# Retention and a routed mixture of experts on one core: the table of slots holds a row number instead of five bfloat16 values

## The chip, the cores and the metric

The kernel runs on one core of a Trainium2 chip. The metric is the device time of one execution in microseconds (us): the median of three timed runs. The profile is one further execution of the same program, recorded by the hardware profiler. Engines are named as the profile names them: PE is TensorE, DVE is VectorE, ACT is ScalarE, POOL is GpSimd, SP is SyncE.

## The reference

Four sequences of 768 tokens go through a retention with 8 heads of 64 columns. Its output, 3072 rows of 512, is the input `x` of a mixture of 8 experts, each with a first product to 1024 columns and a second one back to 512. A noisy gate chooses two experts for every token.

```python
for t in range(S):                                   # retention, per batch and head
    state = gamma * state + outer(k[t], v[t])
    y[t] = scale * q[t] @ state
x = y.transpose(0, 2, 1, 3).reshape(3072, 512)
noisy = x @ w_gate + log1p(exp(x @ w_noise)) * noise
top2 = the two largest of noisy, per token
top2_w = exp(top2_l - max); top2_w /= top2_w.sum(-1) + 1e-09
for e in range(8):
    for k in range(2):
        mask = top2[:, k] == e
        h = maximum(x[mask] @ w1[e], 0)
        out[mask] += top2_w[mask, k] * (h @ w2[e])
```

## The kernel before, in words

**Order of the work.** The order in which the kernel's code issues instructions is the order in which each engine executes them: nothing is moved by a scheduler. An engine that waits for an operand holds everything behind it in its own queue. SP's queue carries most DMAs and the transposes by DMA; POOL's queue carries the indirect DMAs.

**Retention.** It works on 24 chunks of 128 tokens, six per sequence. A chunk's output is scaled by a power of two and split into two float16 parts (`x_split`), which are transposed by DMA for the gate (L346) and written as one row per token to a table in DRAM, `xbuf` (L347: 1024 float16, 2,048 bytes a row).

**Routing.** Each sequence is routed in steps `route_a` to `route_h`, spread over the following chunks; the last sequence has no chunks behind it, and beside its routing stand only the units of expert 0's first list (`early`). The result is a table of slots. An expert has up to seven blocks of 128 slots, and each slot names a token and its gate weight. To fill the table, every token and each of its two choices becomes a one-hot row of lanes (`a`, L470), a one-hot row of blocks (`ob`, L468), and the product `bb` of `ob` with five bfloat16 values `vv`: the token number in two parts and the weight in three (L478). `route_f` sums a^T bb over the tokens on PE into 5 x 56 columns (L485), and `acc` collects them over the sequences. `slots` makes the token `tk`, the row index `idx` and the weight `wacc` from it. `ranks` orders experts 1 to 7 by their number of tokens and permutes `tk` and `wacc`.

**Experts.** For each block, `gather` (L591, on POOL) brings the 128 rows named by `idx` from `xbuf` into one of four buffers `xg`, and `x_t` (L598, on SP) transposes them into `xe`. A first product (`mm1`, "unit" below: 12 matmuls, L672 to L674, for 128 of the 1024 columns and half of the tokens) goes into one of three PSUM buffers `pH`; ACT takes its upper part `hh` (L675), and DVE the rest `hl` (L676), which is the last reader of the buffer. There are sixteen units an expert. Then `mm2` follows block by block (L702 to L704); ACT scales its rows with the gate weight times the inverse scales, `gse` (L688), and `put` (L693, on POOL) adds them to `out` in DRAM by an indirect DMA. Every put waits until the put before it has landed.

**Beside an expert.** While expert e is in its second product, the gathers and transposes of expert e+1 are issued, one block ahead of each `mm2` (for expert 0, the last four units of its first product also take one each). The weights of e+1 are loaded, measured (`w_sum`), scaled (`w_scale`) and split into a high part on ACT (`w_hi`, L192) and a low part on DVE (`w_lo`, L197). Beside expert 0's second product also stand `route_g` and `loop_table` (L534 to L572): tables for a loop at the end, over tokens beyond an expert's slots.

Of the kernel before, what the change touches and what calls it, by code (L numbers as in the profile page):

```python
# [32 lines left out]
# fullest with the most slots.  What exceeds an expert's slots goes through the loop at the end.  # L33
# [23 lines left out]
def _constants():  # L57
# [34 lines left out]
def moe_kernel(ctx, tc, qT, kT, kt, vt, noise, wgn, w1, w2, ctab, qtab, xbuf, out):  # L92
# [9 lines left out]
    # keeps the tensor engine's clock up while the first operands come in  # L102
# [21 lines left out]
    zero = consts.tile([128, DM], F32, name="zero")  # L124
    posb = consts.tile([128, NCH, NL], F32, name="posb")       # place in the list, BIG if not chosen
    gateb = consts.tile([128, NCH, NL], F32, name="gateb")
    acc = consts.tile([128, NV, NCOL], F32, name="acc")    # slots: token + 1 in two parts, weight in three
    wacc = consts.tile([128, NCOL], F32, name="wacc")
    lanes = consts.tile([128, 128], BF, name="lanes")
    blks = consts.tile([128, NCOL], BF, name="blks")  # L130
# [13 lines left out]
    LST = pR[:, 160:160 + NV * NCOL].rearrange("p (v n) -> p v n", v=NV)  # L144
# [18 lines left out]
    def w_load(e, which, i, n=1):  # L163
        # n quarters from the ith on
# [78 lines left out]
    def zero_out(i):  # L243
        # the output and the rows of padding start as zeros
        if i < 6:
            nc.sync.dma_start(out[128 + i * 512:128 + (i + 1) * 512, :].rearrange("(p r) d -> p r d", p=128),
                              zero[:, None, :].to_broadcast([128, 4, DM]))
        else:
            nc.sync.dma_start(out[:128, :], zero)
# [39 lines left out]
    def q_table(c):  # L289
        # the decay of chunk c's queries, out of chunk 0's  # L290
# [48 lines left out]
    def x_split(j, eng=None):  # L339
# [7 lines left out]
        nc.sync.dma_start(xbuf[128 + j * C:128 + (j + 1) * C, :], x.rearrange("p a d -> p (a d)"))  # L347
# [27 lines left out]
    def route_b(b):  # L375
        # noisy logits, the two largest
# [21 lines left out]
        R[b] = (oh, mb, den)  # L398

    def route_c(b):  # L400
        # places in the lists
        oh, mb, den = R[b]
# [6 lines left out]
        g = work.tile([128, 2, NC], F32, name="g")  # L409
# [12 lines left out]
        nc.vector.tensor_tensor(g[:, 1], den, g[:, 0], op=OP.mult)
        R[b] = (oh, g, gr, cb, vv)

    def route_h(b):
        oh, g, gr, cb, vv = R[b]
        nc.vector.tensor_copy(vv[:, :, :, 2], g)
        nc.vector.tensor_tensor(gr, g, vv[:, :, :, 2], op=OP.subtract)
        nc.vector.tensor_copy(vv[:, :, :, 3], gr)
        nc.vector.tensor_tensor(vv[:, :, :, 4], gr, vv[:, :, :, 3], op=OP.subtract)  # L430

    def route_d(b):
        oh, g, gr, cb, vv = R[b]
# [22 lines left out]
        lf = work.tile([128, 2, 2, NC], BF, name="lf")  # L456
        nc.vector.tensor_copy(lf, lb)
        R[b] = (oh, g, ps, lf, vv)

    def route_e(b, k):  # L460
        # the slots' tokens and weights as sums of one-hot products
        if k == 0:
            R[b] += (work.tile([128, 2, NC, 128], BF, name="a", bufs=1),
                     work.tile([128, 2, NC, NV, NCOL], BF, name="bb", bufs=1),
                     work.tile([128, 2, NC, NCOL], BF, name="ob", bufs=1))
        oh, g, ps, lf, vv, a, bb, ob = R[b]
        s3 = [128, NC, NCOL]
        nc.vector.tensor_tensor(ob[:, k], blks[:, None, :].to_broadcast(s3), lf[:, 1, k, :, None].to_broadcast(s3),  # L468
                                op=OP.is_equal)
        nc.vector.tensor_tensor(a[:, k], lanes[:, None, :].to_broadcast([128, NC, 128]),  # L470
                                lf[:, 0, k, :, None].to_broadcast([128, NC, 128]), op=OP.is_equal)
        # the last sequence's are waited for: GpSimd takes a part
        m = 3 if b == B - 1 else NV
# [7 lines left out]
    def route_f(b):  # L481
# [458 lines left out]
```

## Time and profile before

| | |
|---|---|
| median of three runs | 727.25 us |
| lowest and highest of them | 721.35 us, 729.62 us |
| span of the profiled execution | 733.5 us |
| PE busy | 685.0 us, 93% of the span, 4789 instructions |
| DVE busy | 294.0 us, 40%, 719 instructions |
| ACT busy | 311.0 us, 42% |
| POOL busy | 237.9 us, 32% |
| bytes moved by DMA | 119.09 MB |

The page gives no other time of the profiled execution than its span. "Busy" counts an instruction's time on its engine, without waits. A group row of the page reads: line, engine, operation, output <- inputs, count | busy us, mean ns of one | idle time just before, and what ended most of it. A timeline row reads: start in us, duration in us, engine, line, operation, tiles, count, and in brackets the wait before and what ended it. Rows that start with two numbers joined by a colon are stretches of the span.

### The profile page before, as it was taken

What the parts mean: (1) busy time and instruction counts of PE and PEld (TensorE: products, weight loads), DVE (VectorE), ACT (ScalarE), POOL (GpSimd) and SP (SyncE); (2) the same over time, 40 slices, a digit from 0 to 9 for tenths busy, and PEclk for the clock granted to TensorE, in tenths of its full rate; (3) what the DMA queues carried; (4) which work ended last, traced back from release to release, by engine and by line L of the source; (5) the groups of instructions that cost most, each with busy time, mean ns of one, the idle gap of its engine ahead of it and who ended that gap; (6) DMA issues with size and microseconds to landing.
All of it is one profiled execution on the core that took longest, in us unless ns stands there. A gap on an engine that the chain in (4) does not pass through costs nothing.

```text
span 733.5 us, 12009 instructions
## 1 busy us (share of the span) xinstructions
PE 685.0 (93%) x4789; PEld 431.0 (59%) x4789; DVE 294.0 (40%) x719; ACT 311.0 (42%) x562; POOL 237.9 (32%) x186
## 2 busy tenths in 40 slices
PE   8879879889879999999999999999999999999991
PEld 6879769777448555455546545654555466446540
DVE  3326778695942573215221521432152225216100
ACT  4554444447204374344443534443444435344110
POOL 4564734652333220431033123304321421240021
PEclk9997787986999999999999999999999999999997
DMA  9999955995869953467367826744673685353032
GB/s 331 260 296 245 290 181 165 294 294 146 303 115 248 216 163 130 88 115 221 84 115 120 267 45 119 182 155 86 116 218 85 122 177 185 68 104 60 11 47 30
DMA packets 116057, 119.09 MB, mean 162 GB/s; under 512 B 82560, under 2 KB 82816, under 8 KB 112416
## 3 DMA queue, kind: packets, MB, share of 16 engines
q1 hardware_dynamic: 104080, 91.25, 45.0%
q0 software_dynamic: 11344, 26.22, 19.4%
q10 hardware_dynamic: 576, 0.84, 0.4%
q8 instruction: 38, 0.62, 0.4%
q14 instruction: 19, 0.16, 0.1%
HBM read 72.67 MB, written 26.21 MB: 135 GB/s over the span
## 4 chain that ended last, share of the span: by engine, by line
PE 76%; DVE 8%; DMA 7%; ACT 3%; issue 2%; POOL 1%; SPq 1%; POOLq 0%; ACTq 0%
PE pH L672 11%; PE pH L673 11%; PE pH L674 11%; PE pO L702 10%; PE pO L704 10%; PE pO L703 10%; PE pY L320 3%; DMA xt<-x 3%; PE pA L306 2%; PE pY L316 2%; PE pU L324 1%; DMA wst<-w 1%; DVE am L309 1%; DVE bb L478 1%; DMA xe<-xg 1%
## 5 line engine op out<-in xcount | busy, mean ns | idle before, releaser
L693 POOL DMA_INDIRECT out<-ot,idx x54 | 84.9, 1573 | 360.2 <-ACT ot L688 214.4
L672 PE MATMUL pH<-xe,w1h 128*128 128x384 f16 (+4 forms) x544 | 176.6, 325 | 3.9 <-DMA xe<-xg 3.3
L673 PE MATMUL pH<-xe,w1h 128*128 128x384 f16 (+4 forms) x544 | 176.5, 324 | 0.0
L674 PE MATMUL pH<-xe,w1l 128*128 128x384 f16 (+4 forms) x544 | 176.4, 324 | 0.0
L676 DVE SCALAR_TENSOR_TENSOR hl<-pH,hh 128x384 f16<-128x384 f32 (+4 forms) x136 | 74.4, 549 | 210.5 <-ACT hh L675 209.7
L704 PE MATMUL pO<-w2h,hl 128*128 128x512 f16 x384 | 145.5, 379 | 0.0
L703 PE MATMUL pO<-w2l,hh 128*128 128x512 f16 x384 | 145.5, 379 | 0.0
L702 PE MATMUL pO<-w2h,hh 128*128 128x512 f16 x384 | 145.5, 379 | 0.0
L675 ACT ACTIVATE hh<-pH 128x384 f16<-128x384 f32 (+4 forms) x136 | 65.7, 483 | 127.1 <-PE pH L674 125.2
L688 ACT ACTIVATE ot<-pO,gse 128x512 f32<-128x512 f32 (+4 forms) x54 | 37.0, 686 | 173.8 <-PE pO L704 169.3
L197 DVE SCALAR_TENSOR_TENSOR w1l<-wst,wsc,w1h 128x1024 f16<-128x1024 f32 x32 | 42.7, 1339 | 106.8 <-ACT w1h L192 106.8
L672 PEld LDWEIGHTS <-w1h 128*128 128x128 f16 x544 | 54.2, 100 | 34.5 <-DMA xe<-xg 1.7
L673 PEld LDWEIGHTS <-w1h 128*128 128x128 f16 x544 | 53.5, 98 | 35.4 <-issue 2.8
L674 PEld LDWEIGHTS <-w1l 128*128 128x128 f16 x544 | 53.5, 98 | 34.5 <-issue 0.3
L175 ACT ACTIVATE junk<-wst 128x1024 bf16<-128x1024 f32 x64 | 67.1, 1049 | 5.6 <-DMA wst<-w 2.8
L704 PEld LDWEIGHTS <-hl 128*128 128x128 f16 x384 | 37.5, 98 | 45.8 <-DVE hl L676 0.5
L702 PEld LDWEIGHTS <-hh 128*128 128x128 f16 x384 | 38.1, 99 | 44.1
L703 PEld LDWEIGHTS <-hh 128*128 128x128 f16 x384 | 37.5, 98 | 44.2
L591 POOL DMA_INDIRECT xg<-xbuf,idx x54 | 54.7, 1014 | 25.9 <-issue 14.9
L320 PE MATMUL pY<-vp,am 128*128 128x64 f32 x384 | 60.4, 292 | 0.0
L320 PEld LDWEIGHTS pY<-vp,am 128*128 128x128 f32 x384 | 58.1, 220 | 0.6 <-issue 0.2
L344 POOL TENSOR_TENSOR x<-xs,x 128x512 f16<-128x512 f32 x23 | 32.3, 1405 | 58.6 <-issue 32.3
(163 smaller groups left out, 778.1 us busy)
## 6 DMA issues: line engine op xcount, KB each, us to landing
wst<-w SPq DMA_DIRECT2D x28, 1024.0 KB, 9.2
in_q<-qT SPq DMA_DIRECT2D x24, 256.0 KB, 3.7
in_k<-kT SPq DMA_DIRECT2D x24, 256.0 KB, 4.2
in_v<-vt SPq DMA_DIRECT2D x24, 256.0 KB, 4.9
in_kt<-kt SPq DMA_DIRECT2D x24, 256.0 KB, 5.0
xbuf<-x SPq DMA_DIRECT2D x24, 256.0 KB, 2.6
out<-zero SPq DMA_DIRECT2D x6, 1024.0 KB, 12.6
wst<-w SPq DMA_DIRECT2D x8, 512.0 KB, 7.6
```

The lines of the kernel that those rows point to most:

```text
L175: nc.scalar.activation(junk, st[:, i * 1024:(i + 1) * 1024], AF.Square, accum_out=ss[:, i:i + 1])
L320: nc.tensor.matmul(pY[:, 2 * i + s, :], AM[j][:, s, i, :], VP[j][:, 2 * i + s, :], start=(not c and i == 0 and s == 0), stop=True, skip_gr ...
L591: nc.gpsimd.indirect_dma_start(out=x[:n], out_offset=None, in_=xbuf[:128 + B0 * S] if e == 0 and t < 3 else xbuf, in_offset=bass.IndirectO ...
L672: nc.tensor.matmul(p[:, :n], whi, xh, start=(k == 0), stop=False)
L673: nc.tensor.matmul(p[:, :n], whi, xl, start=False, stop=False)
L674: nc.tensor.matmul(p[:, :n], wlo, xh, start=False, stop=(k == KT - 1))
L675: nc.scalar.activation(hh[:, f, n0:n1], p[:, :n], AF.Relu)
L676: nc.vector.scalar_tensor_tensor(hl[:, f, n0:n1], p[:, :n], 0.0, hh[:, f, n0:n1], op0=OP.max, op1=OP.subtract)
L693: nc.gpsimd.indirect_dma_start(out=out, out_offset=bass.IndirectOffsetOnAxis(ap=idx[:n, i:i + 1], axis=0), in_=ot[:n], in_offset=None, com ...
L702: nc.tensor.matmul(p, a, WT["2h"][:, f, :], start=(f == 0), stop=False)
L703: nc.tensor.matmul(p, a, WT["2l"][:, f, :], start=False, stop=False)
L704: nc.tensor.matmul(p, c, WT["2h"][:, f, :], start=False, stop=(f == FT - 1))
```

## The change

The table of slots now holds one float16 number per slot: the token's row, as a constant of the kernel (token minus 1536, plus 1 where that is not negative, so that no token has 0). `ob` is the one-hot of blocks times that number, made by one tensor_scalar per chunk; `a` likewise is one tensor_scalar per chunk. The values `vv`, the product `bb`, `wacc`, `acc` and the table `gateb` are gone, and the matmuls of `route_f` have 56 columns instead of 280.

The weights take another way. A row of `xbuf` gets four more float32 numbers behind x: the token's two gate weights and its two experts' numbers, so that a row has 2,064 bytes. `route_h` writes them for a sequence with one DMA on SP. A gather brings them along with x, and a new step, `weight`, compares the two expert numbers with the block's expert and sums the weights that match; it is one DVE instruction per block, issued in `x_t` behind the transpose. `out_scale` reads its result `gw` where it read `wacc`.

```diff
-NV = 5
+XW = DM + 4
...
     def route_h(b):
-        oh, g, gr, cb, vv = R[b]
-        nc.vector.tensor_copy(vv[:, :, :, 2], g)
-        nc.vector.tensor_tensor(gr, g, vv[:, :, :, 2], op=OP.subtract)
-        nc.vector.tensor_copy(vv[:, :, :, 3], gr)
-        nc.vector.tensor_tensor(vv[:, :, :, 4], gr, vv[:, :, :, 3], op=OP.subtract)
+        oh, mb, den, i8, g, dn, cb = R[b]
+        nc.vector.tensor_tensor(g[:, :, 0], dn, invx[:, b * NC:(b + 1) * NC], op=OP.mult)
+        nc.vector.tensor_tensor(g[:, :, 1], den, g[:, :, 0], op=OP.mult)
+        nc.vector.tensor_copy(g[:, :, 2:4], i8[:, :, 0:2])
+        if b >= B0:
+            l8 = work.tile([128, NC, 2], F32, name="l8")
+            nc.vector.tensor_scalar(l8, g[:, :, 2:4], float(E), -float(E), op0=OP.is_equal, op1=OP.mult)
+            nc.vector.tensor_tensor(g[:, :, 2:4], g[:, :, 2:4], l8, op=OP.add)
+        nc.sync.dma_start(xbuf[128 + b * S:128 + (b + 1) * S, DM:].rearrange("(c p) d -> p c d", p=128), g)
...
     def route_e(b, k):
-        nc.vector.tensor_tensor(ob[:, k], blks[:, None, :].to_broadcast(s3), lf[:, 1, k, :, None].to_broadcast(s3),
-                                op=OP.is_equal)
-        nc.vector.tensor_tensor(a[:, k], lanes[:, None, :].to_broadcast([128, NC, 128]),
-                                lf[:, 0, k, :, None].to_broadcast([128, NC, 128]), op=OP.is_equal)
...
-                eng.tensor_tensor(bb[:, k, :, v], ob[:, k, :, None, :].to_broadcast(s4),
-                                  vv[:, k, :, v, None].to_broadcast(s4), op=OP.mult)
+        for c in range(NC):
+            nc.vector.tensor_scalar(ob[:, k, c], blks, lf[:, 1, k, c:c + 1], row[:, b * NC + c:b * NC + c + 1],
+                                    op0=OP.is_equal, op1=OP.mult)
+        for c in range(NC):
+            nc.vector.tensor_scalar(a[:, k, c], lanes, lf[:, 0, k, c:c + 1], None, op0=OP.is_equal)
...
-        x = XP[0].tile([128, 2 * DM], F16, name="xg", bufs=4)
+        x = XP[0].tile([128, XW], F32, name="xg", bufs=4)
...
+    def weight(x, n, ef, out):
+        g = x[:n, DM:]
+        t = work.tile([128, 2], F32, name="wt2")
+        nc.vector.scalar_tensor_tensor(t[:n], g[:, 2:4], ef[:n], g[:, 0:2], op0=OP.is_equal, op1=OP.mult,
+                                       accum_out=out[:n])
...
     def x_t(e, t):
         o, n, i = block(e, t)
-        nc.sync.dma_start_transpose(XE[e][:, :, o:o + n], XG.pop((e, t))[:n])
+        x = XG.pop((e, t))
+        nc.sync.dma_start_transpose(XE[e][:, :, o:o + n], x[:n, :DM].bitcast(F16))
+        if t == 0:
+            GW[e] = work.tile([128, NBLK], F32, name="gw")
+            nc.gpsimd.memset(GW[e], 0.0)
+        weight(x, n, eidf[:, e:e + 1], GW[e][:, t:t + 1])
...
-        nc.vector.tensor_scalar(GS[e][:, n0:n1], wacc[:, NBLK * e + n0:NBLK * e + n1], i2, None, op0=OP.mult)
+        nc.vector.tensor_scalar(GS[e][:, n0:n1], GW[e][:, n0:n1], i2, None, op0=OP.mult)
```

Beside this, `rows_of` has one instruction more (the sign), `ranks` permutes `tk` alone and keeps the experts' numbers in float32 (`eidf`) for `weight`, `route_g` makes one table instead of two, `loop_table` has one cast more, and the loop at the end takes its weights from the gathered rows too.

The first place is DVE's order from expert 1 to expert 2, before. `hl` is the first product's rest, the four small instructions behind it are the weights' scale, `w1l` the low part of expert 2's weights; the three `hl` at the end are the first of expert 2.

```order
L676 SCALAR_TENSOR_TENSOR hl<-pH,hh 128x416 x8
L181 TENSOR_REDUCE s_3357<-pR 128x1
L152 TENSOR_SCALAR p2m<-s_3357 128x1
L153 TENSOR_SCALAR wsc_3141<-p2m 128x1
L155 TENSOR_SCALAR wsc_3141<-p2m 128x1
L197 SCALAR_TENSOR_TENSOR w1l<-wst_3139,wsc_3141,w1h 128x1024 x4
L676 SCALAR_TENSOR_TENSOR hl<-pH,hh 128x416 x3
```

The same place after the change, from behind the weights' scale on. `wt` and `gw` are the outputs of `weight`, which reads the gathered rows `xg`.

```order
L580 SCALAR_TENSOR_TENSOR wt_3434,gw<-xg,eidf 128x2
L580 SCALAR_TENSOR_TENSOR wt_3468,gw<-xg,eidf 128x2
L198 SCALAR_TENSOR_TENSOR w1l<-wst_3204,wsc_3206,w1h 128x1024
L580 SCALAR_TENSOR_TENSOR wt_3503,gw<-xg,eidf 128x2
L198 SCALAR_TENSOR_TENSOR w1l<-wst_3204,wsc_3206,w1h 128x1024
L580 SCALAR_TENSOR_TENSOR wt_3539,gw<-xg,eidf 128x2
L198 SCALAR_TENSOR_TENSOR w1l<-wst_3204,wsc_3206,w1h 128x1024
L580 SCALAR_TENSOR_TENSOR wt_3575,gw<-xg,eidf 128x2
L198 SCALAR_TENSOR_TENSOR w1l<-wst_3204,wsc_3206,w1h 128x1024
L580 SCALAR_TENSOR_TENSOR wt_3610,gw<-xg,eidf 128x2
L580 SCALAR_TENSOR_TENSOR wt_3644,gw<-xg,eidf 48x2
L669 SCALAR_TENSOR_TENSOR hl<-pH,hh 128x416 x3
```

Seven instructions that read a gathered block now stand between the last `hl` of expert 1 and the first of expert 2, among the four `w1l`.

The second place is DVE's order in the last sequence's routing, before, for its two lists: `lf` holds every token's lane and block, and `acc` collects the table.

```order
L457 CAST lf<-lb 128x24
L468 TENSOR_TENSOR ob<-blks,lf 128x336
L470 TENSOR_TENSOR a<-lanes,lf 128x768
L478 TENSOR_TENSOR bb<-ob,vv 128x6x168
L676 SCALAR_TENSOR_TENSOR hl<-pH,hh 128x384 x2
L468 TENSOR_TENSOR ob<-blks,lf 128x336
L470 TENSOR_TENSOR a<-lanes,lf 128x768
L478 TENSOR_TENSOR bb<-ob,vv 128x6x168
L490 TENSOR_TENSOR acc<-acc,pR 128x280
```

The same place after the change, up to the first weights of expert 0's second list:

```order
L456 CAST lf<-lb 128x24
L467 TENSOR_SCALAR ob<-blks,lf,ct 128x56 x6
L470 TENSOR_SCALAR a<-lanes,lf 128x128 x6
L669 SCALAR_TENSOR_TENSOR hl<-pH,hh 128x384 x2
L467 TENSOR_SCALAR ob<-blks,lf,ct 128x56 x6
L470 TENSOR_SCALAR a<-lanes,lf 128x128 x6
L481 TENSOR_TENSOR tk<-tk,pR 128x56
L487 TENSOR_SCALAR padv<-tk,ct 128x4
L488 SCALAR_TENSOR_TENSOR padv<-tk,padv 128x4
L489 SCALAR_TENSOR_TENSOR idx<-tk,padv 128x4
L580 SCALAR_TENSOR_TENSOR wt_2446,gw<-xg,eidf 128x2
```

Three wide instructions a list have become twelve small ones, and instructions that read gathered rows follow `idx`.

The third place is SP's order behind the last chunk, before: its transpose and its row write, the fills of `out` with zeros, and the transposes of expert 0's second list.

```order
L346 DMA_TRANSPOSE xt<-x_2069 128x8x128
L347 DMA xbuf<-x_2069 128x1024
L246 DMA out<-zero 512x1x512 x6
L249 DMA out<-zero 128x512
L598 DMA_TRANSPOSE xe<-xg 128x8x128 x3
```

After the change:

```order
L347 DMA_TRANSPOSE xt<-x_2108 128x8x128
L348 DMA xbuf<-x_2108 128x1024
L429 DMA xbuf<-g 128x6x4
L247 DMA out<-zero 512x1x512 x6
L250 DMA out<-zero 128x512
L586 DMA_TRANSPOSE xe<-xg 128x8x128 x3
```

The write of the last sequence's weights and expert numbers (`g`) stands ahead of the fills.

More of the change, by code (lines that the diff above doesn't have):

```diff
@@ L73, in _constants @@
     put("tok1", np.arange(NCH)[None, :] * C + p[:, None] + 1)
-    tv = np.zeros((128, NCH, 2))
-    tv[:, :, 0], tv[:, :, 1] = p[:, None] + 1, np.arange(NCH)[None, :] * C
-    put("tokv", tv.reshape(128, NCH * 2))
+    tk = np.arange(NCH)[None, :] * C + p[:, None] - N // 2
+    put("row", np.where(tk < 0, tk, tk + 1))
     put("pad", p[:, None] - 127)
+    put("lane", p[:, None] - (127 + N // 2))
     put("i64", np.arange(64)[None, :])
@@ L123, in moe_kernel @@
     onef = consts.tile([128, 128], F32, name="onef")
-    zero = consts.tile([128, DM], F32, name="zero")
+    zero = consts.tile([128, DM + 4], F32, name="zero")
     posb = consts.tile([128, NCH, NL], F32, name="posb")
[L126 to L130, printed above, removed]
+    tk = consts.tile([128, NCOL], F32, name="tk")
+    lanes = consts.tile([128, 128], F16, name="lanes")
+    blks = consts.tile([128, NCOL], F16, name="blks")
     idx = consts.tile([128, NCOL], I32, name="idx")
@@ L246, in zero_out @@
             nc.sync.dma_start(out[128 + i * 512:128 + (i + 1) * 512, :].rearrange("(p r) d -> p r d", p=128),
-                              zero[:, None, :].to_broadcast([128, 4, DM]))
+                              zero[:, None, :DM].to_broadcast([128, 4, DM]))
         else:
-            nc.sync.dma_start(out[:128, :], zero)
+            nc.sync.dma_start(out[:128, :], zero[:, :DM])
     gss = work.tile([128, 1], F32, name="gss")
@@ L397, in route_b @@
         nc.vector.tensor_tensor(den, m8[:, :, 1], m8[:, :, 0], op=OP.subtract)
-        R[b] = (oh, mb, den)
+        R[b] = (oh, mb, den, i8)
     def route_c(b):
-        oh, mb, den = R[b]
+        oh, mb, den, i8 = R[b]
         nc.scalar.activation(den, den, AF.Exp)
@@ L481, in route_f @@
+        oh, ps, lf, a, ob = R[b]
+        row = K("row")
+        for c in range(NC):
[3 more added lines that the diff above has]
+            nc.vector.tensor_scalar(a[:, k, c], lanes, lf[:, 0, k, c:c + 1], None, op0=OP.is_equal)
     def route_f(b):
-        oh, g, ps, lf, vv, a, bb, ob = R[b]
+        oh, ps, lf, a, ob = R[b]
         for k in range(2):
@@ L484, in route_f @@
             for c in range(NC):
-                nc.tensor.matmul(LST, a[:, k, c, :], bb[:, k, c], start=(k == 0 and c == 0),
+                nc.tensor.matmul(LST, a[:, k, c, :], ob[:, k, c], start=(k == 0 and c == 0),
                                  stop=(k == 1 and c == NC - 1), skip_group_check=True)
         if b == 0:
-            nc.vector.tensor_copy(acc, LST)
+            nc.vector.tensor_copy(tk, LST)
         else:
-            nc.vector.tensor_tensor(acc, acc, LST, op=OP.add)
-    tk = consts.tile([128, NCOL], F32, name="tk")
@@ L494, in slots, with rows_of @@
-    def slots(n0, n1):
-        nc.vector.tensor_tensor(tk[:, n0:n1], acc[:, 0, n0:n1], acc[:, 1, n0:n1], op=OP.add)
-        if n0 < NBLK:
-            rows_of(tk, n0, n1)
-        nc.vector.tensor_tensor(wacc[:, n0:n1], acc[:, 3, n0:n1], acc[:, 4, n0:n1], op=OP.add)
-        nc.vector.tensor_tensor(wacc[:, n0:n1], wacc[:, n0:n1], acc[:, 2, n0:n1], op=OP.add)
-    def rows_of(tk, n0, n1):
+            nc.vector.tensor_tensor(tk, tk, LST, op=OP.add)
+    def rows_of(n0, n1):
         padv = work.tile([128, NCOL], F32, name="padv")
-        nc.vector.tensor_scalar(padv[:, n0:n1], tk[:, n0:n1], 0.0, K("pad"), op0=OP.is_equal, op1=OP.mult)
-        nc.vector.scalar_tensor_tensor(idx[:, n0:n1], tk[:, n0:n1], 127.0, padv[:, n0:n1], op0=OP.add, op1=OP.add)
+        t, u = tk[:, n0:n1], padv[:, n0:n1]
+        nc.vector.tensor_scalar(u, t, 0.0, K("lane"), op0=OP.is_equal, op1=OP.mult)
+        nc.vector.scalar_tensor_tensor(u, t, 0.0, u, op0=OP.is_lt, op1=OP.add)
+        nc.vector.scalar_tensor_tensor(idx[:, n0:n1], t, float(127 + N // 2), u, op0=OP.add, op1=OP.add)
@@ L570, in loop_table @@
         nc.vector.tensor_scalar(le, loop_e, float(E), -float(E), op0=OP.is_equal, op1=OP.mult)
[L571 removed]
+        nc.vector.tensor_tensor(loop_x, loop_e, le, op=OP.add)
+        nc.vector.tensor_copy(loop_i[:, :64], loop_x)
         nc.vector.tensor_copy(loop_i[:, 64:65], cs[:, NL - 1:NL])
@@ L626, in moe_kernel @@
         at(NC * (B0 + 1) + 2 + t // 2, x_t, 0, t)
-    at(1, nc.sync.dma_start, xbuf[:128, :], zero.bitcast(F16))
+    at(1, nc.sync.dma_start, xbuf[:128, :], zero)
+    at(1, nc.vector.memset, eidf[:, 0:1], 0.0)
     v_scale(0)
@@ L872, in moe_kernel @@
         for c in range(NCH):
-            nc.tensor.matmul(pl, a[:, c, :], rr[:, c, :], start=(c == 0), stop=(c == NCH - 1))
+            nc.tensor.matmul(pl[:, 0:1], a[:, c, :], K("tok1")[:, c:c + 1], start=(c == 0), stop=(c == NCH - 1))
         pv = work.tile([128, 2], F32, name="pv")
```

79 lines of the change are left out of this document (30 added, 49 removed).

## The prediction

> **What bounds the kernel now.** I read the page first, then a table by stage, then the waits, and last the timeline at the places where one expert follows another.
>
> ```profile
> span 733.5 us, 12009 instructions
> PE 685.0 (93%) x4789; PEld 431.0 (59%) x4789; DVE 294.0 (40%) x719; ACT 311.0 (42%) x562; POOL 237.9 (32%) x186
> PE 76%; DVE 8%; DMA 7%; ACT 3%; issue 2%; POOL 1%; SPq 1%; POOLq 0%; ACTq 0%
> ```
>
> TensorE (PE) is the bound by share, VectorE (DVE) is free 60% of the time. The shares hide two stages: retention and routing up to about 217 us, where PE waits now and then, and the experts behind it. The second stage in the table by stage (columns: length, busy us of PE, PEld, DVE, ACT, POOL with counts, granted clock, DMA share, GB/s):
>
> ```profile
> 290.00:327.00 37.00, 36.96 (x261) 18.86 (x259) 6.17 (x9) 13.44 (x21) 13.25 (x10) 1.00 0.51 90
> 327.00:357.00 30.00, 30.00 (x178) 17.24 (x177) 13.81 (x25) 15.46 (x27) 4.96 (x4) 1.00 0.75 200
> ```
>
> The first row is a second product, the next a first product: PE has no gap, at full clock. So time taken off DVE here buys nothing, and whatever makes PE wait is added whole. Three rows of the waits (total us, times, longest) say what could:
>
> ```profile
> SPq L598 <- DMA xg<-xbuf,idx: 316.9, 41, 23.4
> POOL out L693 <- DMA out<-ot,idx: 93.1, 24, 6.5
> PE pH L672 <- DVE hl L676: 0.5, 1, 0.5
> ```
>
> SyncE's queue waits 317 us for gathered rows to land before it transposes them. Nobody minds: SyncE has nothing urgent behind them. GpSimd's queue alternates put, gather, put, gather, and each put waits for the landing of the put before, so gathers run late. The last row is the lever: PE can wait for DVE's `hl`, because a unit of the first product needs one of three PSUM buffers, and `hl` (L676) is the last reader that frees it.
>
> **What the change adds at each change of expert.** The new `weight` is issued by `x_t` right behind the transpose, so a DVE instruction now waits for the landing that only SyncE waited for. DVE's queue runs in order; in the order rows, all seven weights of expert e+1 stand ahead of the first `hl` of e+1. When do these landings come? From expert 1 to 2:
>
> ```profile
> 329.78 0.94 POOL L591 DMA_INDIRECT xg<-xbuf,idx  x1 [0.30 <-issue]
> ...
> 334.39 1.19 SPq L598 DMA_TRANSPOSE xe<-xg  x1
> ...
> 327.42 0.59 DVE L676 SCALAR_TENSOR_TENSOR hl<-pH,hh 128x416 f16<-128x416 f32 x1 [12.99 <-ACT hh L675]
> ...
> 331.47 0.34 PE L672 MATMUL pH<-xe,w1h 128*128 128x416 f16 x1
> ```
>
> The seventh gather is issued at 329.78 and its transpose at 334.39, which I read as its landing. Expert 2's first `hl` ran at 327.42; its fourth unit, the first that reuses a buffer, began on PE at 331.47. After the change this `hl` waits until 334.39, plus one weight: 0.25 us, an estimate (two-input instructions with few columns take 0.16 to 0.23, rows of the routing below; an accumulator is read besides). The buffer is free at 334.39 + 0.25 + 0.59 = 335.23, and PE waits 335.23 - 331.47 = 3.8 us. The same pair at the later boundaries (`hl` 0.57, then 0.56, since the shapes shrink):
>
> ```profile
> 403.29 1.18 SPq L598 DMA_TRANSPOSE xe<-xg  x1
> 398.63 0.33 PE L672 MATMUL pH<-xe,w1h 128*128 128x400 f16 x1
> ...
> 468.90 1.18 SPq L598 DMA_TRANSPOSE xe<-xg  x1
> 465.66 0.33 PE L672 MATMUL pH<-xe,w1h 128*128 128x400 f16 x1
> ...
> 536.94 1.14 SPq L598 DMA_TRANSPOSE xe<-xg  x1
> 532.77 0.33 PE L672 MATMUL pH<-xe,w1h 128*128 128x400 f16 x1
> ...
> 596.94 1.23 SPq L598 DMA_TRANSPOSE xe<-xg  x1
> 598.95 0.32 PE L672 MATMUL pH<-xe,w1h 128*128 128x384 f16 x1
> ...
> 663.28 1.23 SPq L598 DMA_TRANSPOSE xe<-xg  x1
> 661.50 0.32 PE L672 MATMUL pH<-xe,w1h 128*128 128x384 f16 x1
> ```
>
> Adding 0.82 (0.81 for the last two) to the landing and taking off the unit's start gives 5.5, 4.1, 5.0, 0 and 2.6 us. Expert 6 escapes because it has six blocks beside seven of expert 5, so its last gather goes out a block earlier. These five and the 3.8 above: 21.0 us.
>
> From expert 0 to 1 two things stand behind the last weight: the last low part of the weights `w1l`, and the tables of the loop (L539 to L572).
>
> ```profile
> 249.72 2.48 DVE L197 SCALAR_TENSOR_TENSOR w1l<-wst,wsc,w1h 128x1024 f16<-128x1024 f32 x2 [2.72 <-ACT w1h L192]
> ...
> 254.36 0.16 DVE L549 TENSOR_TENSOR cnt<-cum,capd 128x9 f32<-128x9 f32 x1
> ...
> 261.40 0.15 DVE L572 CAST loop_i<-cs 128x1 int32<-128x1 f32 x1
> ...
> 258.80 1.19 SPq L598 DMA_TRANSPOSE xe<-xg  x1
> ...
> 255.99 0.34 PE L672 MATMUL pH<-xe,w1h 128*128 128x416 f16 x1
> ...
> 262.90 0.34 PE L672 MATMUL pH<-xe,w1h 128*128 128x416 f16 x1
> ```
>
> The landing at 258.80, a weight (0.25) and one `w1l` (2.48 / 2 = 1.24) give 260.3. PE began the unit at 255.99 and needs that part for its last matmul, some 1.9 us in (the first three units last from 255.99 to 262.90, 2.3 us each with the small matmuls of `w_scale` among them): 2.4 us of wait. Then `route_g` (2.2 us from the end of the two `w1l` at 252.20 to 254.36; two of its five instructions go, the largest among them: 1.3) and the table (254.36 to 261.55: 7.2, and 0.2 for one more cast): first `hl` from 269.0 to 269.6. The fourth unit wanted 262.90 + 2.4 = 265.3: 4.3 more. Together 6.7 us. **All boundaries: 21.0 + 6.7 = 27.7 us.** Should gathers land 1 us earlier, it is some 21; 1 us later, some 34.
>
> **What it takes off the routing.** Per list, `ob`, `a` and the product `bb` become twelve small tensor_scalar instructions. In the last sequence's routing, which PE does wait for:
>
> ```profile
> 189.47 0.23 DVE L683 TENSOR_SCALAR gse<-wacc,i 128x3 f32<-128x3 f32 x1
> 189.61 1.48 DVE L676 SCALAR_TENSOR_TENSOR hl<-pH,hh 128x384 f16<-128x384 f32 x3
> ...
> 191.64 0.17 DVE L422 TENSOR_TENSOR g<-den,g 128x6 f32<-128x6 f32 x1
> ...
> 194.50 0.51 DVE L468 TENSOR_TENSOR ob<-blks,lf 128x336 bf16<-128x336 bf16 x1
> 194.92 0.95 DVE L470 TENSOR_TENSOR a<-lanes,lf 128x768 bf16<-128x768 bf16 x1
> 195.79 2.32 DVE L478 TENSOR_TENSOR bb<-ob,vv 128x1008 bf16<-128x1008 bf16 x1
> ```
>
> Before: 194.50 to the end of `bb` at 198.11, 3.6 us a list. A tensor_scalar with a pointer lasts 0.23 and lets the next start after 0.14 (189.47 to 189.61): twelve cost 1.7 to 2.8 us. Two lists gain 1.6 to 3.8; I take 2.5, towards the lower price, since they depend on nothing among themselves.
>
> [...]
>
> But the gain meets a queue. SyncE's order now has the write of `g` ahead of the fills of `out` with zeros:
>
> ```profile
> 179.30 7.86 SPq L246 DMA_DIRECT2D out<-zero  x6
> ...
> 195.00:200.00 5.00, 4.95 (x26) 2.25 (x25) 5.00 (x7) 0.29 (x1) 2.36 (x2) 1.00 0.60 222
> 200.00:205.00 5.00, 2.77 (x18) 1.47 (x16) 3.88 (x10) 0.40 (x1) 1.57 (x2) 1.00 0.00 0
> ...
> 204.93 0.98 POOL L591 DMA_INDIRECT xg<-xbuf,idx  x1 [3.43 <-DVE wacc L499]
> ...
> 208.90 7.36 SPq L598 DMA_TRANSPOSE xe<-xg  x4
> ```
>
> The fills were issued from 179.30 on, and in the table by stage DMA is at rest from 200 on: some 20 us, with nothing behind them. `g` is ready near 192.3 (the row at 191.64 and three more small ones), so the fills start 13 us later and drain until about 212; gathers now meet them, and the transposes, ready at about 206.5, queue behind them in place of 208.90 freely. [...] I take 0 for the last routing: between -4 (the gain stays) and +4.
>
> For the three sequences routed beside the retention the same instructions go (and the small `vv` steps). What the chain holds of them:
>
> ```profile
> PE pH L672 11%; PE pH L673 11%; PE pH L674 11%; PE pO L702 10%; PE pO L704 10%; PE pO L703 10%; PE pY L320 3%; DMA xt<-x 3%; PE pA L306 2%; PE pY L316 2%; PE pU L324 1%; DMA wst<-w 1%; DVE am L309 1%; DVE bb L478 1%; DMA xe<-xg 1%
> ```
>
> `bb` has 1%, some 7 us for eight lists, of which the two of the last routing (2 x 2.32) take the most. I take -2 for the rest, between -5 and 0, for the weights of expert 0 wait on DVE there too. The 16-byte writes of `g`, the rows of 2,064 bytes in place of 2,048 and the shorter matmuls (56 columns for 280) I cost at nothing: beside a gather of some 5 us they are small. If the longer rows cost a gather 1 us, that is the upper bound above. `ranks` now starts after the gathers; the loads behind it waited for the transposes before.
>
> **Sum.** 27.7 + 0 - 2 = 26 us on the profiled 733.5, so 759.5. That execution is slower than the three runs (721.35 to 729.62, median 727.25; the page gives its span and no more), so I carry the difference over: 727 + 26 = **753 us**. Bounds: 21 - 9 = +12 (739) and 34 + 4 = +38 (765).
>
> **Rivals.** (1) *The landings don't reach PE.* At the boundaries the covers are two units of the first product. What decides is the put chain's lag: if the last gather lands 4 to 5 us sooner than now, every wait above is zero, as at expert 6. For it: longer mm2 phases or quicker puts would do it; against it: 24 waits of puts for puts. [...] (2) *Longer rows hurt more:* gathers of 2,064 bytes land 2 us or more later, five boundaries pay it all, expert 6 and the first in part: 753 + 12 = 765. For it: every gather moves; against it: 16 bytes are under 1%. (3) *The fills delay the start of the experts* by the whole 13 us: 753 + 13 = 766. Against it: DMA was at rest from 200 to 205, so part of the fills finds room.
>
> **Chances.** Forecast 0.67, rival 1 0.20, rival 2 0.07, rival 3 0.06. The range 738 to 767 holds the forecast with its bounds and rivals 2 and 3 mostly, and leaves out rival 1 and a rest. About 1% (7 us) is what a measurement can tell from no change: rival 1 splits into 0.08 faster and 0.12 within 1%; with 0.03 for small sums of the forecast's case, 0.15 within 1% and 0.77 slower.
>
> **What would show it.** Right: DVE's `hl` behind weights with waits of 5 to 8 us for the gather at each boundary but that of expert 6; PE idle 3 to 6 us there, released by `hl`; expert 0 to 1 two idles. Routing: `ob` and `a` at 1.7 to 2.8 us a list, fills of `out` at 192. Wrong: PE without gaps in these stages, or gathers that land before the first product starts.

## The result and the profile after

The changed kernel takes 770.04 us (median of five runs, 768.56 to 776.62) where the kernel before, on the same chip, takes 729.62 (five runs): 1.061 times as long, with a 95% interval of 1.055 to 1.068. The direction was forecast; the size was 40 us instead of 26, and 770 lies outside the range of 738 to 767.

From the page of the changed kernel: the span, the engines' busy time, the chain of waits by engine, and two groups (busy us, mean ns | idle time just before, and what ended most of it).

```profile
span 774.8 us, 12223 instructions
PE 693.7 (90%) x4789; PEld 434.4 (56%) x4789; DVE 296.5 (38%) x873; ACT 311.3 (40%) x562; POOL 225.9 (29%) x192
PE 40%; DMA 25%; issue 17%; DVE 11%; ACT 3%; POOL 1%; SPq 1%; POOLq 0%; DVEq 0%; ACTq 0%
...
L665 PE MATMUL pH<-xe,w1h 128*128 128x384 f16 (+4 forms) x544 | 181.7, 334 | 32.6 <-DVE hl L669 25.0
...
L580 DVE SCALAR_TENSOR_TENSOR wt<-xg,eidf 128x2 f32<-128x2 f32 (+4 forms) x54 | 11.8, 219 | 241.7 <-DMA xg<-xbuf,idx 241.7
```

The chain, three quarters PE before, is now PE for 40%. The rest is DMA (25%, of which the page gives 19% to the landings of the puts, `out<-ot,idx`), issue (17%, time in which an engine waited for nothing that the profile shows) and DVE (11%). At the change from expert 1 to 2 it runs from the landing of one put to the next (324.09 to 347.80), beside PE, so its shares don't price what PE loses. The link is seen in the groups and the waits: the group of `weight` (L580) is busy for 12 us and waits for 242, and the waits of the changed kernel have PE at the end of the same link (total us, times, longest):

```profile
DVE wt L580 <- DMA xg<-xbuf,idx: 241.7, 44, 10.9
PE pH L665 <- DVE hl L669: 25.0, 7, 5.8
PE pH L667 <- DVE w1l L198: 7.2, 4, 4.9
```

The same change of expert that the prediction worked through, 1 to 2, in the timeline after:

```profile
339.81 0.22 DVE L580 SCALAR_TENSOR_TENSOR wt<-xg,eidf 128x2 f32<-128x2 f32 x1 [6.46 <-DMA xg<-xbuf,idx]
...
345.22 0.21 DVE L580 SCALAR_TENSOR_TENSOR wt<-xg,eidf 48x2 f32<-48x2 f32 x1 [5.18 <-DMA xg<-xbuf,idx]
...
345.37 1.57 DVE L669 SCALAR_TENSOR_TENSOR hl<-pH,hh 128x416 f16<-128x416 f32 x3
```

The seventh `weight` waits until 345.22, and then three `hl` run at once: they had been ready one after the other while DVE stood in front of them. These are all waits of PE at the changes of expert, from 0 to 1 (four), 1 to 2, 2 to 3, 3 to 4, 4 to 5, and 6 to 7 (two small ones):

```profile
256.05 0.35 PE L667 MATMUL pH<-xe,w1l 128*128 128x416 f16 x1 [0.83 <-DVE w1l L198]
257.24 0.35 PE L667 MATMUL pH<-xe,w1l 128*128 128x416 f16 x1 [0.49 <-DVE w1l L198]
262.88 0.53 PE L667 MATMUL pH<-xe,w1l 128*128 128x416 f16 x1 [4.94 <-DVE w1l L198]
271.75 0.34 PE L665 MATMUL pH<-xe,w1h 128*128 128x416 f16 x1 [1.42 <-DVE hl L669]
346.00 0.51 PE L665 MATMUL pH<-xe,w1h 128*128 128x416 f16 x1 [5.75 <-DVE hl L669]
420.50 0.49 PE L665 MATMUL pH<-xe,w1h 128*128 128x400 f16 x1 [5.54 <-DVE hl L669]
493.77 0.49 PE L665 MATMUL pH<-xe,w1h 128*128 128x400 f16 x1 [4.43 <-DVE hl L669]
569.25 0.49 PE L665 MATMUL pH<-xe,w1h 128*128 128x400 f16 x1 [5.74 <-DVE hl L669]
697.21 0.34 PE L667 MATMUL pH<-xe,w1l 128*128 128x384 f16 x1 [0.91 <-DVE w1l L198]
703.13 0.32 PE L665 MATMUL pH<-xe,w1h 128*128 128x384 f16 x1 [1.57 <-DVE hl L669]
```

Look at the second column too. A matmul of 400 or 416 columns took 0.33 to 0.34 us before; behind the long waits it takes 0.49 to 0.53. The table by stage (length, busy us of PE, PEld, DVE, ACT, POOL, then the granted clock, the DMA share and GB/s) shows why, first behind five long waits, then behind a short one:

```profile
346.00:350.00 4.00, 4.00 (x13) 1.77 (x13) 1.77 (x8) 0.00 (x0) 0.84 (x2) 0.55 0.93 211
420.50:424.00 3.50, 3.50 (x11) 1.57 (x11) 1.74 (x8) 0.00 (x0) 1.15 (x3) 0.50 0.78 166
493.80:497.30 3.50, 3.50 (x11) 1.54 (x11) 1.70 (x8) 0.00 (x0) 2.01 (x3) 0.50 0.71 157
569.30:572.80 3.50, 3.50 (x11) 1.53 (x11) 1.69 (x8) 0.00 (x0) 1.91 (x3) 0.50 0.68 162
262.90:266.90 4.00, 4.00 (x14) 2.04 (x15) 3.38 (x21) 1.20 (x2) 1.37 (x1) 0.50 0.88 252
703.00:706.00 3.00, 2.87 (x18) 1.75 (x18) 2.03 (x10) 0.72 (x2) 0.41 (x1) 1.00 0.90 119
```

After these waits of 4.4 to 5.8 us PE works at half its clock (0.50 to 0.55) for some microseconds; after the one of 1.6 us it doesn't (1.00). PE is counted as busy all that time (4.00 of 4.00 us in the first row), so the busy share hides it.

By stages, from the first matmul of each first product to the next one's, in the two timelines (us; the waits are the rows above):

| stage | before | after | more | of it PE's waits | rest |
|---|---|---|---|---|---|
| up to expert 0's first unit | 176.3 | 171.0 | -5.3 | | |
| expert 0's first list, last routing | 40.9 | 43.9 | +3.0 | | |
| expert 0's second list | 38.8 | 39.3 | +0.5 | | |
| expert 1 | 68.6 | 79.0 | +10.4 | 7.7 | 2.7 |
| expert 2 | 67.3 | 75.0 | +7.7 | 5.8 | 1.9 |
| expert 3 | 67.1 | 74.4 | +7.3 | 5.5 | 1.8 |
| expert 4 | 67.1 | 74.2 | +7.1 | 4.4 | 2.7 |
| expert 5 | 66.4 | 74.6 | +8.2 | 5.7 | 2.5 |
| expert 6 | 63.0 | 63.0 | 0.0 | 0.0 | 0.0 |
| expert 7 and the end | 78.0 | 80.5 | +2.5 | 2.5 | 0.0 |

The experts' stages give 43.2 us: 31.6 us of waits, and 11.6 us beside them, which fall to the five stages with a long wait; by the rows above they are the matmuls at half the clock. The first row alone is no finding. Over the executions of this record that moment lies between 169 and 176 us in the five with the old routing and between 166 and 173 in eight with the new; the means differ by 2.0 us (172.5 and 170.5), less than the scatter.

The last routing, after. The two lists' one-hots `ob` (L467) and `a` (L470) on DVE, the write of `g` and the fills on SP, the first gather of the second list on POOL, its transposes, and PE's first matmul on them:

```profile
191.23 1.32 DVE L467 TENSOR_SCALAR ob<-blks,lf,ct 128x56 f16<-128x56 f16 x6
192.46 1.07 DVE L470 TENSOR_SCALAR a<-lanes,lf 128x128 f16<-128x128 f16 x6
...
189.42 0.37 SPq L429 DMA_DIRECT2D xbuf<-g  x1
189.84 7.22 SPq L247 DMA_DIRECT2D out<-zero  x6
...
198.10 0.98 POOL L571 DMA_INDIRECT xg<-xbuf,idx  x1 [14.87 <-DVE idx L489]
...
206.17 9.29 SPq L586 DMA_TRANSPOSE xe<-xg  x4
...
214.87 0.40 PE L665 MATMUL pH<-xe,w1h 128*128 128x256 f16 x1 [7.59 <-DMA xe<-xg]
```

A list takes 2.2 us on DVE (191.23 to 193.44, when the next `hl` starts) instead of 3.6. But the gather needs 8.1 us from issue to the first transpose, where it needed 4.0 before (204.93 to 208.90), and PE waits 7.6 us for the transposes instead of 3.3. Between the two lie the fills.

### The profile page after: what moved, and what is told of

It is laid out like the page before. It is cut to its first block, busy times and chain, and to the rows that moved or that the text cites. A ratio compares the mean times of both kernels' runs of the same rounds, so it can differ in the third digit from the quotient of the medians.

```text
span 774.8 us, 12223 instructions
## 1 busy us (share of the span) xinstructions
PE 693.7 (90%) x4789; PEld 434.4 (56%) x4789; DVE 296.5 (38%) x873; ACT 311.3 (40%) x562; POOL 225.9 (29%) x192
## 4 chain that ended last, share of the span: by engine, by line
PE 40%; DMA 25%; issue 17%; DVE 11%; ACT 3%; POOL 1%; SPq 1%; POOLq 0%; DVEq 0%; ACTq 0%
DMA out<-ot,idx 19%; PE pH L665 6%; PE pH L666 6%; PE pH L667 6%; PE pO L695 4%; PE pO L697 4%; PE pO L696 4%; DMA xg<-xbuf,idx 3%; PE pY L321 3%; DVE a L470 2%; DVE am L310 2%; PE pA L307 2%; PE pY L317 2%; PE pU L325 2%; DMA xt<-x 1%
## 5 line engine op out<-in xcount | busy, mean ns | idle before, releaser
L665 PE MATMUL pH<-xe,w1h 128*128 128x384 f16 (+4 forms) x544 | 181.7, 334 | 32.6 <-DVE hl L669 25.0
L667 PE MATMUL pH<-xe,w1l 128*128 128x384 f16 (+4 forms) x544 | 181.3, 333 | 7.2 <-DVE w1l L198 7.2
L666 PE MATMUL pH<-xe,w1h 128*128 128x384 f16 (+4 forms) x544 | 181.5, 334 | 0.0
L580 DVE SCALAR_TENSOR_TENSOR wt<-xg,eidf 128x2 f32<-128x2 f32 (+4 forms) x54 | 11.8, 219 | 241.7 <-DMA xg<-xbuf,idx 241.7
L666 PEld LDWEIGHTS <-w1h 128*128 128x128 f16 x544 | 54.6, 100 | 60.9 <-issue 29.5
L665 PEld LDWEIGHTS <-w1h 128*128 128x128 f16 x544 | 55.2, 101 | 43.4 <-DMA xe<-xg 8.1
L176 ACT ACTIVATE junk<-wst 128x1024 bf16<-128x1024 f32 x64 | 67.1, 1049 | 5.4 <-DMA wst<-w 5.2
L321 PE MATMUL pY<-vp,am 128*128 128x64 f32 x384 | 62.2, 298 | 0.0
L321 PEld LDWEIGHTS pY<-vp,am 128*128 128x128 f32 x384 | 60.1, 227 | 0.6 <-issue 0.2
L345 POOL TENSOR_TENSOR x<-xs,x 128x512 f16<-128x512 f32 x23 | 26.9, 1168 | 63.0 <-issue 30.5
```

What stands on the lines that cost most here:

```text
L176: nc.scalar.activation(junk, st[:, i * 1024:(i + 1) * 1024], AF.Square, accum_out=ss[:, i:i + 1])
L321: nc.tensor.matmul(pY[:, 2 * i + s, :], AM[j][:, s, i, :], VP[j][:, 2 * i + s, :], start=(not c and i == 0 and s == 0), stop=True, skip_gr ...
L665: nc.tensor.matmul(p[:, :n], whi, xh, start=(k == 0), stop=False)
L666: nc.tensor.matmul(p[:, :n], whi, xl, start=False, stop=False)
L667: nc.tensor.matmul(p[:, :n], wlo, xh, start=False, stop=(k == KT - 1))
```

## The experiments

Theory Q: the wait at the head of DVE's queue keeps `hl` back, PE stalls for want of a PSUM buffer, and then runs at half its clock. Rival R: the landings themselves come late, through longer rows, 16-byte writes and later fills. The first four kernels below were to tell them apart and to price the clock.

**Take the wait away (const).**

```diff
-        weight(x, n, eidf[:, e:e + 1], GW[e][:, t:t + 1])
+        weight(zero, n, eidf[:, e:e + 1], GW[e][:, t:t + 1])
```

> The kernel after, but each weight instruction reads a constant tile of zeros instead of the gathered block, so that it waits for no landing; everything else stands (gate weights are left out, the output is zero). Theory Q (the wait at the head of DVE's queue keeps hl back, PE then stalls and afterwards runs some microseconds at half the clock): the stalls at the changes of expert go, 31 us of them and 9 us of slow clock, so about 730 us, between 725 and 736, and no wait of PE for hl. Rival R (the landings themselves came late, through longer rows, 16-byte writes and later fills, and the wait only shows it): 760 us or more, with PE then waiting for the transposed rows.

Measured: 732.89 us, 1.002 times before (0.998 to 1.005). The kernel leaves out the gate weights, so its output is zero; longer rows, writes of `g`, later fills and all 54 `weight` instructions are still there, and the whole loss is gone. Rival R falls.

**Move the wait back (late).** `x_t` only notes the `weight`. It is issued three blocks later, and the rest behind the tenth unit of the expert's own first product, for `n` counts from 0 (for expert 0's second list, behind `ranks`):

```diff
-        weight(x, n, eidf[:, e:e + 1], GW[e][:, t:t + 1])
+        PEND.append(lambda: weight(x, n, eidf[:, e:e + 1], GW[e][:, t:t + 1]))
+        weights(3 if e or t > 2 else 0)
...
     ranks()
+    weights(0)
...
                     if n == 2:
                         w_scale(e, "2")
+                    if n == 9:
+                        weights(0)
                         out_scale(e, 0, NBLK)
```

> The kernel after, with the weight instructions moved back in DVE's order: three blocks later than the gather, and the last three of an expert behind the ninth unit of its own first product, with the output scale behind them. Theory Q: 730 us, between 725 and 738, as without the wait. Rival R: 760 or more.

Measured: 732.40 us, 1.002 times before (0.998 to 1.006). The waits of PE in this kernel that bear on the matter:

```profile
PE pH L672 <- DMA xe<-xg: 5.9, 1, 5.9
PE pH L672 <- DVE hl L676: 1.2, 2, 0.6
```

The waits for `hl` fall from 25.0 to 1.2 us though every `weight` still reads its gathered block: only its place in DVE's queue has changed. One wait of 5.9 us is left, that for the transposes of expert 0's second list; the experiments on the fills take it up.

**Add the wait alone to the kernel before (before_wait, and again as before_wait2).**

```diff
-        nc.sync.dma_start_transpose(XE[e][:, :, o:o + n], XG.pop((e, t))[:n])
+        x = XG.pop((e, t))
+        nc.sync.dma_start_transpose(XE[e][:, :, o:o + n], x[:n])
+        w2 = work.tile([128, 2], F32, name="wt2")
+        nc.vector.tensor_copy(w2[:n], x[:n, :2])
```

> The kernel before, with one small DVE copy of two numbers of each gathered block, issued behind its transpose where the changed kernel has its weight instruction; nothing else. Theory Q: it takes most of the loss by itself: 36 to 42 us more than before, 763 to 770 us. Rival R: within 6 us of before.

Measured: 754.01 us, 1.033 times before (1.026 to 1.040). The wait alone makes the kernel slower, clearly, but by 23 us and not by 36 to 42. Its table by stage, behind PE's waits for experts 2 to 5:

```profile
339.00:343.00 4.00, 3.90 (x12) 1.76 (x12) 1.86 (x9) 0.00 (x0) 0.76 (x1) 0.50 0.95 209
410.60:414.00 3.40, 3.40 (x21) 1.97 (x21) 2.40 (x9) 1.17 (x2) 1.69 (x2) 1.00 0.75 171
480.00:484.00 4.00, 3.58 (x13) 1.75 (x13) 2.22 (x9) 0.00 (x0) 2.36 (x2) 0.63 0.45 125
551.00:554.00 3.00, 2.96 (x18) 1.74 (x18) 2.03 (x9) 0.73 (x2) 2.23 (x2) 1.00 0.46 90
```

Here PE had waited 3.3, 1.65, 2.6 and 1.65 us, since the last gathers landed 7.7 to 9.3 us behind the start of the first products and not 10.4 to 11.9 as in the changed kernel (the start of the last transpose is taken as the landing, here and below). The clock fell behind the first and the third wait (0.50, 0.63) and not behind the two of 1.65 (1.00). Before these two, at experts 3 and 5, the landings came 3.8 and 4.0 us earlier than in the changed kernel, and the stages took 68.8 and 68.2 us instead of 74.4 and 74.6: the earlier landing saved as much of wait, and 1.8 and 2.5 us more with the clock at full speed.

**Keep PE busy through the stall (after_busy).**

```diff
                if e:
+                    if n == 2 and 2 <= e <= 5:
+                        busy(20)
```

> The kernel after, with twenty matmuls on a constant behind the third unit of the first product of experts 2 to 5, so that PE is idle for less than 2 us there (they take about 4.3 us of a stall of 4.4 to 5.8 us). If the clock falls because PE stands still, the four units behind the stalls keep the full clock, 1.75 us each: 7 us less than after, some 763 us. If the slow units have another cause (the DMA traffic at the same time), the same 770 us, or up to 3 more.

Measured: 766.21 us, 1.048 times before (1.041 to 1.055): 4 us less than the changed kernel where it was first measured, and within the interval of its repeat below, so the time doesn't decide. The profile says more. At the places of the stalls of experts 3 and 4:

```profile
420.00:422.00 2.00, 2.00 (x14) 1.14 (x13) 0.58 (x1) 1.53 (x2) 0.00 (x1) 1.00 0.94 291
...
493.00:495.00 2.00, 2.00 (x8) 0.88 (x7) 0.30 (x2) 0.56 (x2) 0.42 (x2) 0.50 0.95 314
```

At experts 2, 3 and 5 the clock stayed full (1.00), with DMA as busy as in the changed kernel (0.94 of its engines in the first row). The stages of experts 3 and 5 took 71.4 and 71.0 us instead of 74.4 and 74.6, but their last gathers also landed 1.5 and 0.9 us earlier; expert 2's gained 0.6 though its last gather landed 1.0 us later. With the landings allowed for, the full clock was worth 1.5, 2.7 and 1.6 us there, an estimate from these stages and landings. At expert 4 the landing came 1.8 us later and the clock fell (0.50 in the second row), although PE stood still for only 1.9 us behind the dummies, while 2.4 us at expert 2 left it full (1.00). So in these rows the stall, not the traffic, takes the clock away; how long a stall does so is not settled: in before_wait 2.6 us had done it (0.63).

**The longer rows (before_rows_wait, and again as before_rows2).** The first kernel with the wait, and in addition:

```diff
-    xbuf = nc.dram_tensor("xbuf", [N + 128, 2 * DM], F16, kind="Internal").ap()
+    xbuf = nc.dram_tensor("xbuf", [N + 128, 2 * DM + 8], F16, kind="Internal").ap()
...
-        x = XP[0].tile([128, 2 * DM], F16, name="xg", bufs=4)
+        x = XP[0].tile([128, 2 * DM + 8], F16, name="xg", bufs=4)
...
+        nc.sync.dma_start(xbuf[128 + b * S:128 + (b + 1) * S, 2 * DM:].rearrange("(c p) d -> p c d", p=128),
+                          zero[:, :4 * NC].bitcast(F16).rearrange("p (c d) -> p c d", d=8))
```

> The kernel before with the small DVE copy of each gathered block (as in before_wait) and with rows of 2,064 bytes: the gathers bring 16 bytes more a row, and the 16-byte pieces of every sequence are written by a DMA as in the changed kernel (zeros here). The wait alone cost 23 us, and in its profile the last gathers landed 8 us behind the start of a first product, against 11 to 12 in the changed kernel. If the longer rows make the landings late once something waits for them: 765 to 772 us, landings 10 to 12 us behind the start. If rows play no part and the put chain alone sets it: 752 to 757, landings as in before_wait.

Measured: 762.19 us, 1.045 times before (1.040 to 1.050), with landings 9.8 to 12.2 us behind the start. That looked like a price of the rows, but the two kernels had been measured on different chips. So both were run again beside the changed kernel on one chip:

> The changed kernel as it is, beside the next three on one chip, so that their differences can be taken. If the step of the put chain that its first profile showed (6.3 to 8.4 us between puts of an expert) belongs to the kernel and not to one execution, the last gathers of experts 2 to 5 again land 10 to 12 us behind the start of their first product; 6.1% slower than before.

> The kernel before with the small DVE copy of each gathered block, once more, beside the changed kernel on one chip. If its earlier landings belong to the kernel: again 7.7 to 9.3 us behind the start and about 3.3% over before. If they were chance: 10 to 12 us and 4.5 to 5% over before.

> The same with rows of 2,064 bytes and the 16-byte writes, once more. If the longer rows cost something of their own: 8 us or more over before_wait2. If not: the same within 4 us.

Measured, against the same runs of before: 1.052 (1.042 to 1.063) for the change, 1.039 (1.030 to 1.048) for the wait alone, 1.048 (1.038 to 1.059) for wait and rows. PE's waits of the two:

```profile
PE pH L675 <- DVE hl L679: 15.8, 8, 4.4
...
PE pH L677 <- DVE hl L681: 23.4, 8, 5.0
```

The order is that of the first measurements, and three quarters of the change's loss here (3.9 of 5.2%) belongs to the wait alone. The rest between the kernels lies inside the intervals. The landings of experts 2 to 5 were 7.6 to 9.5 us behind the start without the longer rows and 7.3 to 11.2 with them, and single boundaries jump by 3 to 5 us from one execution to the next; in const, whose rows are long as well, they were 7.7 to 10.9, no later than the 9.8 to 11.4 of the kernel before. Whether the longer rows make the landings late stays open.

**The fills (late_fill, late_fill_act, after_fill).** The seven `zero_out` go back in front of the write of `g`:

```diff
+    for i in range(7):
+        zero_out(i)
     route_c(b)
     route_h(b)
...
-    for i in range(7):
-        zero_out(i)
     route_f(b)
```

> The kernel late (weights moved back in DVE's order), with the fills of the output issued behind the last chunk, ahead of the write of g as in the kernel before. If the fills ate the gain of the routing: the last gathers of expert 0 land some 4 us after issue instead of 8, and 3 to 5 us less than late, 727 to 730 us where late has 732. If g, now behind the fills, lands as late as they drain: 732 or more.

> As late_fill, with the last sequence's g written from ScalarE's queue instead of SyncE's, so that it doesn't stand behind the fills. If a queue is taken in order, g lands earlier than in late_fill and the gathers are issued earlier: 1 to 3 us less than late_fill, 725 to 728. If the DMA engines' load sets it, the same as late_fill.

> The changed kernel with the fills of the output ahead of the write of g, as late_fill has them, and the weights where the change put them. Between late and late_fill this was worth 10 to 12 us. If the two costs add up, some 10 us less than the changed kernel, 758 to 762 us, with PE's wait ahead of expert 0's second list gone and the stalls at the changes of expert as before. If the stalls only take over what the fills give back: 765 or more.

Measured: late_fill 719.96 us, 0.986 times before (0.981 to 0.991), the version that beats both kernels. Over late, at 1.002, that is 1.6% or some 11 us, where 3 to 5 were expected. late_fill_act 722.55 us, 0.994 (0.991 to 0.998). after_fill 760.61 us, 1.046 (1.035 to 1.056), against 766.56 for the change beside it. In late_fill PE waits for `hl` 0.5 us and for `xe` not at all:

```profile
PE pH L672 <- DVE hl L676: 0.5, 1, 0.5
```

Its stage of expert 0's first list and the last routing takes 36.2 us (late 43.9, before 40.9), that of the second list 36.9 (38.6, 38.8). after_fill has the same two stages short (37.1 and 36.9) and the experts' waits much as in the change (`hl` 21.5 us, where it had 25.0). In the profile, then, the two costs add, as the first of the two expectations had it, and the fills were worth some 7 us of the first of these stages; the two times, 1.046 and 1.052, are too near each other to show it, and the 6 us between them are fewer than the 10 expected. With them out of the way the stage is 3.8 to 4.7 us shorter than before the change: more than the 2.8 of the shorter lists.

From which queue `g` was written made no gain. In late_fill, from SyncE behind the fills, and in late_fill_act, from ScalarE, with the first gather that waits for it:

```profile
189.11 0.38 SPq L429 DMA_DIRECT2D xbuf<-g  x1
197.78 0.98 POOL L571 DMA_INDIRECT xg<-xbuf,idx  x1 [14.87 <-DVE idx L489]
```

```profile
188.20 0.39 ACTq L429 DMA_DIRECT2D xbuf<-g  x1
196.87 0.98 POOL L571 DMA_INDIRECT xg<-xbuf,idx  x1 [14.87 <-DVE idx L489]
```

8.7 us lie between the two rows in both: the gather is released by `idx`, not by `g`.

**The one-hots of the first three sequences (late_fill_tt).**

```diff
-        for c in range(NC):
+        if b < B - 1:
+            nc.vector.tensor_tensor(a[:, k], lanes[:, None, :].to_broadcast([128, NC, 128]),
+                                    lf[:, 0, k, :, None].to_broadcast([128, NC, 128]), op=OP.is_equal)
+        for c in range(NC if b == B - 1 else 0):
```

> The kernel late_fill, with the one-hots of lanes of the first three sequences made by one tensor_tensor a list, as before the change, since many of the small tensor_scalar instructions took 1.1 to 1.3 us there instead of 0.24, each until a GpSimd tensor operation ended. If those waits lie on the path: 3 to 8 us less than late_fill, 712 to 717. If the retention hides them: the same ratio to before as late_fill (0.986), or a little more, since a tensor_tensor of 768 columns takes 0.95 us and slows GpSimd.

Measured: 719.53 us, 0.985 times before (0.979 to 0.990): no difference from late_fill that could be measured. If these waits cost time on the path, it is less than the 5 us or so that the intervals leave room for.

## Why the prediction was wrong in size and right in kind

- **The mechanism held.** `weight` at the head of DVE's queue, `hl` late, PE without a PSUM buffer: const and late, which touch nothing else, bring the time back to that of before. Expert 6 escapes, as forecast, because its last gather lands 4.1 us behind the start.
- **The waits were sized well.** Forecast from the trace of before: 6.7, 3.8, 5.5, 4.1, 5.0, 0 and 2.6 us, 27.7 in all. Measured: 7.7, 5.8, 5.5, 4.4, 5.7, 0 and 2.5, 31.6. The difference of 3.9 is within the bound of "1 us later, some 34", and it follows the landings: at experts 2 to 5 they came 2.1, 0.1, 0.5 and 0.9 us later behind the start than before. The change from 0 to 1 came near by luck: 2.4 us of wait for `w1l` and 4.3 for `hl` were forecast, 6.3 and 1.4 were measured. Its last gather landed 7.2 us behind the start and not 2.8, so PE stood still in the first unit and then ran at half its clock (0.50 from 262.90 to 266.90) while DVE worked off the loop's tables. The gather had gone out at 257.76, behind a put that had waited 7.9 us; what held that put is not shown.
- **The step that failed is the sum at the boundaries.** "Adding 0.82 to the landing and taking off the unit's start" priced the time until PE may start again, and took for granted that it starts at full speed. Here it starts at half (0.50), and the stages with the five waits of 4.4 to 5.8 us cost 11.6 us more. This term was missing from the sum and from the bounds; with it the boundaries come to 39 us from the forecast waits, and to 43 as measured. Without it, the measured waits and routing would have stayed inside the range (727 + 31.6 + 3.5, and the 2 taken off for the retention: 760). The trace of before had shown it at the one place where PE waited for 3.3 us, ahead of 217.20 (clock 0.65):

```profile
217.20:220.60 3.40, 3.40 (x21) 2.62 (x21) 0.42 (x1) 0.38 (x1) 1.57 (x1) 0.65 0.53 84
```

  In the experts' stages waits of 1.4 to 1.65 us left the clock full (1.00 behind 271.75 and 703.13 in the changed kernel, and behind both waits of 1.65 us in before_wait). The waits of 3.3 us and more in the rows above lowered it, to 0.50 to 0.65 over the next 3.4 to 4 us. Between them it went either way: 1.9 us behind the dummies of expert 4 (after_busy, 0.50) and 2.6 us (before_wait, 0.63) lowered it, 2.4 us behind the dummies of expert 2 (after_busy, 1.00) did not. It was full again 3.4 us after the resumption at 346.00, though only 5.9 us after that at 493.77. The runs show no one length of stall and no one length of recovery; what five long waits cost here is the 11.6 us.
- **The routing, taken as 0 between -4 and +4,** came to +3.5 us (3.0 and 0.5) in the profile. Both halves of the argument were there: a list is cheaper by 1.4 us, two by 2.8 (taken: 2.5), and the fills eat it. What the fills cost was worth more than the 2.5 set against them: moving them gave 7 us in this stage alone. That the transposes themselves stand behind the fills, as this 0 took it, no run shows: from the first transpose to PE's first matmul 8.7 us passed (206.17 to 214.87), where before it was 8.3 (208.90 to 217.20). What took longer were the gathers, 8.1 us from issue to the first transpose instead of 4.0. Rival 3, the fills' delay of the experts by 13 us, was thus half right in size, as a cost that hid a gain.
- **The price of tensor_scalar.** The rows above show 2.2 us for twelve instructions, within the 1.7 to 2.8 that the trace's own small instructions gave.
- **The retention, taken as -2,** can't be told: the start of expert 0's first unit came 2.0 us earlier in the mean with the new routing, but it scatters over some 7 us between executions of either kind.
- **Rival 1** (the landings don't reach PE) is out: at five of seven boundaries they reach it by 4 us or more. **Rival 2** (longer rows make gathers 2 us later) is neither shown nor excluded: const, with long rows and no wait, has landings no later than before.

## What to carry to other kernels

An instruction that reads what a DMA brings belongs in an engine's order where the DMA has surely landed, not where the transfer is issued: here `weight`, at the head of DVE's queue, made everything behind it wait, though it is busy for only 0.22 us, and moving it back three blocks and half a product took this kernel from 1.061 to 1.002 times the time before. A wait on TensorE has to be priced with the slow microseconds behind it (11.6 us beside 31.6 us of waits here), which count as busy time and show in the granted clock (0.50). And when a small write is put ahead of a large one in a queue, ask what the large one will now run into.

## What the runs showed of the hardware

- In the experts' stages the clock fell behind waits of 3.3 us and more (0.50 to 0.65) and not behind waits of 1.4 to 1.65 (1.00); between, at 1.9, 2.4 and 2.6 us, it went either way (0.50, 1.00, 0.63); a unit of the first product then took 3.9 us (from 346.00) instead of 2.1. Dummy matmuls kept it up at three of four places (1.00 at experts 2, 3 and 5, 0.50 at expert 4).
- The one-hots `a`, tensor_scalar on float16 with one pointer, take 0.25 us alone, and 0.16 in a row. In the retention of the changed kernel 14 of 36 took 1.07 to 1.30 us. One of them, and the GpSimd operations beside it:

```profile
77.59 1.18 DVE L470 TENSOR_SCALAR a<-lanes,lf 128x128 f16<-128x128 f16 x1
...
77.47 1.24 POOL L345 TENSOR_TENSOR x<-xs,x 128x512 f16<-128x512 f32 x1 [2.02 <-issue]
...
78.68 1.04 POOL L281 TENSOR_TENSOR vp<-in_v,ct 128x512 f32<-128x512 f32 x1
```

  It ends at 78.77, right behind the end of POOL's operation at 78.71, and the next ones end with POOL's next ones: all 14 end 0.05 us behind the end of a GpSimd operation. No run took the GpSimd operations away, so what holds them is not shown. late_fill_tt (0.985 times before, late_fill 0.986) showed that these waits cost this kernel nothing that can be measured.
- `ob`, with two pointers, takes 0.20 us in a row for 56 columns, more than `a` for 128.
